# Attention on one core: score matmuls issued once, an order set by clocks kept for each engine, and a score tile read by two engines at once

## The chip, the cores and the metric

The kernel runs on one core of a Trainium2 chip. Its time is the device time of one execution in microseconds (us). Six runs of the kernel before gave a median of 2381.01 us, from 2344.32 to 2416.8. In what follows PE is the matrix engine, ACT is ScalarE, DVE is VectorE, POOL is GpSimd and SP the engine that issues most transfers.

## The reference

The input has 2048 rows of width 640. Two attention layers and two token-mixing layers alternate, each behind a layer norm and with a residual:

```python
def _A_ref(x, wqkv, wo):             # H = 32 heads, Dh = 20
    q, k, v = split_heads(x @ wqkv)
    scores = jnp.einsum("bhqd,bhkd->bhqk", q, k) * (Dh ** -0.5)
    p = softmax(scores, axis=-1)
    o = jnp.einsum("bhqk,bhkd->bhqd", p, v)
    return merge_heads(o) @ wo

def _B_ref(x, w1, b1, w2, b2):       # mixes along the 2048 rows, F = 1536
    u = gelu(jnp.einsum("bsd,sf->bdf", layernorm(x), w1) + b1)
    return (jnp.einsum("bdf,fs->bds", u, w2) + b2).transpose(0, 2, 1)

x = A_x
for _ in range(2):
    x = x + _A_ref(layernorm(x), A_wqkv, A_wo)
    x = x + _B_ref(layernorm(x), B_w1, B_b1, B_w2, B_b2)
```

The scores are the bulk of the work: 32 heads of 2048 by 2048 numbers in each layer, every one of which passes through an exponential.

## The kernel before

**Stages.** A prologue normalizes the input and projects V and the first keys and queries. Then come `attention` (line 247), the mixer's two halves `mixer_mm1` and `mixer_mm2` (lines 767 and 833), and the same three again for the second layer.

**A layer's attention.** Heads go in 8 groups of four (`g`), queries in 4 blocks of 512 (`qb`), keys in 16 blocks of 128 (`kt`). One *chunk* is the 128 x 512 scores of one head for one key block and one query block; it fills one PSUM bank. There are 2048 chunks, 64 for each of the 32 pairs of a query block and a head group; such a set of 64 is called a *group* below. Three chunks make a *score tile* `S` of three banks (683 tiles in a layer), and there are two such tiles (`sps`, line 251). The other two banks hold `acc`, which gathers probabilities times V for the running group (line 252), and `misc`, for all other matmuls (line 253).

For each tile the loop at lines 742 to 752 records, in this order: the score matmuls of the tile after it (`emit_S`, line 344), the exponential of this tile (`emit_exp`, line 415), some waiting work of DVE (`dve_run`, line 292), the matmuls with V that may go (`pv_ready`, line 675; called PV below), and some matmuls of the *fills* (`emit_fills`, line 714). Fills are all the other work that PE has to do under cover of the exponentials: projections of later keys and queries (line 230), the output projection (lines 553 and 587), and three quarters of the mixer's first product (line 525), whose partial sums are added up in DRAM by POOL's transfers (`uacc`, line 537). One fill group gathers in `misc` and is then copied out by DVE. The order in which the calls are made is the order of the instructions on PE (a chain, line 74) and on DVE (`manual_schedule`, line 740); ACT's exponentials follow it too.

**Two ways to take an exponential.** ACT takes whole tiles: one instruction at line 422 over two or three banks. For some tiles `want_dve` (line 360) leaves the third bank to DVE, which copies it scaled out of PSUM (`tp`, line 430) and, when two such chunks are there, runs five more instructions over both (lines 383 to 397) that build the exponential's bits in `PD`. Such a tile is called a *shared* tile here. A small model in the recording code, with clocks `act` and `dve` and costs in us written beside each operation, decides which tiles are shared and when DVE's waiting operations are recorded.

**What the score matmuls do.** A score matmul contracts over 20 of 32 rows, so heads sit in four strips of 32 rows of the array. Line 745 issues the three matmuls of each tile two or three times over, with the same operands and the same result:

```python
emit_S(t + 1, 2 if fill_queue or fill_state["cur"] else 3)
```

**At the end of a group** the finished `acc` is transposed by DVE out of PSUM (`T1`, line 445), which frees it for the next group, then divided by the row sums and transposed back (lines 452 to 459).

## Time and profile before

| what | value |
|---|---|
| median of 6 runs | 2381.01 us |
| the profiled execution | 2377.39 us, of which 2375.6 us lie between its first and last instruction |
| PE busy | 2095.8 us, 88% |
| ACT busy | 1827.6 us, 77% |
| DVE busy | 1590.7 us, 67% |
| mean granted PE clock | 0.925 of full speed |
| transfers | mean 41 GB/s |

In a profile a row names a line of the code, the engine, the operation, the tile written and the tile read, a count, the busy time and the mean of one, and then the time that the engine stood idle just before these instructions with what ended the wait. A busy PE is not PE at its best: matmuls overlap, and their ends are modelled, so the distance from one start to the next says what a matmul costs. The granted clock is the share of PE's full clock that its throttle let through.

### The profile page before, as it was taken

How to read it: one execution, taken by the hardware profiler on the slowest of the kernel's cores; microseconds unless marked ns; L12 is line 12 of the kernel's file. 1: busy time of each engine (PE TensorE's matmuls, PEld its weight loads, DVE VectorE, ACT ScalarE, POOL GpSimd, SP SyncE). 2: the span in 40 equal slices, each digit the busy share in tenths (PEclk: the TensorE clock that was granted, in tenths of full speed). 3: DMA queues.
4: the chain of work that ended last, by engine and by line, in shares of the span. 5: the costliest groups of instructions: out<-in, count | busy, mean ns of one | idle time of the engine just before them, and what ended most of it. 6: DMA issues, size and time to landing. Idle time of an engine off the chain costs nothing.

```text
span 2375.6 us, 41164 instructions
## 1 busy us (share of the span) xinstructions
PE 2095.8 (88%) x17114; PEld 644.7 (27%) x17284; DVE 1590.7 (67%) x2735; ACT 1827.6 (77%) x1504; POOL 157.0 (7%) x218
## 2 busy tenths in 40 slices
PE   7999999889888988888999899998998899888879
PEld 3222222222222222222542222222222222222235
DVE  6767777777656576656667677777566656766763
ACT  5888888888868787875358888888688677878862
POOL 2000001100120002000000000010001200021000
PEclk9999999999989799986999999999589867999989
DMA  4000002100240014103610000120002400132035
GB/s 115 1 1 1 1 16 73 47 1 21 55 73 1 1 40 70 16 1 99 211 54 1 1 1 1 41 80 27 1 17 65 78 1 1 45 64 33 1 111 174
DMA packets 90779, 97.47 MB, mean 41 GB/s; under 512 B 9696, under 2 KB 68192, under 8 KB 90592
## 3 DMA queue, kind: packets, MB, share of 16 engines
q1 hardware_dynamic: 70464, 71.22, 9.6%
q0 software_dynamic: 20128, 23.62, 6.3%
q8 instruction: 135, 2.21, 0.4%
q14 instruction: 52, 0.43, 0.1%
HBM read 55.48 MB, written 39.32 MB: 40 GB/s over the span
## 4 chain that ended last, share of the span: by engine, by line
PE 42%; ACT 19%; DVE 19%; issue 15%; POOL 4%; DMA 1%; ACTq 0%; POOLq 0%; SPq 0%; another core or an unknown queue 0%; DVEq 0%
PE S L340 20%; ACT P L422 19%; PE acc L654 9%; DVE tp L430 6%; PE y L879 4%; PE misc L230 3%; DVE PD L397 3%; PE misc L553 2%; PE pp L221 2%; POOL uacc_65 L537 1%; POOL uacc_66 L537 1%; PE big L808 1%; PE misc L525 1%; DVE KT L616 1%; DVE x1last L601 1%
## 5 line engine op out<-in xcount | busy, mean ns | idle before, releaser
L422 ACT ACTIVATE P<-S 128x1536 bf16<-128x1536 f32 (+1 forms) x1366 | 1735.6, 1313 | 384.9 <-PE S L340 372.9
L340 PE MATMUL S<-QTq,KT 32*128 32x512 bf16 x10020 | 1055.5, 409 | 138.2 <-DVE tp L430 93.1
L654 PE MATMUL acc<-P,Vaug 128*32 128x512 bf16 x3646 | 589.1, 413 | 35.7 <-DVE T_24414 L445 2.8
L340 PEld LDWEIGHTS <-KT 32*128 32x128 bf16 x10020 | 270.1, 95 | 654.0 <-issue 585.4
L430 DVE TENSOR_SCALAR tp<-S 128x512 f32<-128x512 f32 x450 | 307.0, 683 | 162.6 <-ACT P L422 160.9
L654 PEld LDWEIGHTS <-Vaug 128*32 128x32 bf16 x4096 | 146.4, 94 | 680.8 <-issue 679.8
L172 POOL TENSOR_TENSOR rstd<-veps,mhalf 128x1 f32<-128x1 f32 x64 | 41.7, 652 | 1807.4 <-DVE veps L167 1683.4
L532 DVE COPY ustg<-misc 128x512 f32<-128x512 f32 (+1 forms) x144 | 70.3, 488 | 130.0 <-PE misc L525 50.9
L525 PE MATMUL misc<-h2st,w1st 128*128 128x128 bf16 (+1 forms) x540 | 113.8, 310 | 35.9 <-DVE ustg L532 34.5
L654 PE MATMUL acc<-PD,Vaug 128*32 128x512 bf16 x450 | 116.6, 414 | 2.4 <-DVE PD L397 0.7
L879 PE MATMUL y<-uT,w2s 128*128 128x128 bf16 (+1 forms) x754 | 106.8, 297 | 3.1 <-ACT uT L822 2.4
L230 PE MATMUL misc<-hh,wq_pad 128*128 128x512 bf16 x278 | 90.3, 386 | 7.3 <-DVE QTq L616 4.5
L230 PE MATMUL misc<-hh,wk_pad 128*128 128x512 bf16 x240 | 79.2, 387 | 11.6 <-DVE KT L616 7.5
L553 PE MATMUL misc<-wo_pad,attnT 128*128 128x128 bf16 (+1 forms) x361 | 72.6, 299 | 2.5 <-issue 1.3
L879 PEld LDWEIGHTS <-w2s 128*128 128x128 bf16 x768 | 59.7, 98 | 48.9 <-issue 4.1
L525 PEld LDWEIGHTS <-w1st 128*128 128x128 bf16 x576 | 36.3, 98 | 101.9 <-issue 101.8
L616 DVE CAST QTq<-misc 128x512 bf16<-128x512 f32 x62 | 42.7, 688 | 18.7 <-PE misc L230 13.4
L84 ACT CAST Vaug<-pp 128x500 bf16<-128x500 f32 (+1 forms) x32 | 14.4, 454 | 53.0 <-PE pp L221 52.9
L221 PE MATMUL pp<-wv,hh 128*128 128x500 bf16 (+1 forms) x320 | 52.4, 315 | 1.7 <-DVE hh L86 1.7
L881 DVE SCALAR_TENSOR_TENSOR x2s<-y,b_t,x1in 128x512 f32<-128x512 f32 (+1 forms) x48 | 24.3, 548 | 42.0 <-PE y L879 24.6
L537 POOL DMA_DIRECT2D uacc_66<-ustg x48 | 42.9, 949 | 122.1 <-DVE ustg L532 121.9
L537 POOL DMA_DIRECT2D uacc_65<-ustg x48 | 42.5, 927 | 117.4 <-DVE ustg L532 117.2
(1518 smaller groups left out, 1582.8 us busy)
## 6 DMA issues: line engine op xcount, KB each, us to landing
w2s<-in_B_w_dram SPq DMA_DIRECT2D x16, 768.0 KB
w1st<-in_B_w_dram SPq DMA_DIRECT2D x36, 256.0 KB
uacc_65<-ustg POOLq DMA_DIRECT2D x36, 256.0 KB, 4.0
uacc_66<-ustg POOLq DMA_DIRECT2D x36, 256.0 KB, 4.1
xd_63<-x1s SPq DMA_DIRECT2D x24, 320.0 KB
x1in<-xd_63 SPq DMA_DIRECT2D x24, 320.0 KB
xd_64<-x2s SPq DMA_DIRECT2D x16, 320.0 KB
xin<-xd_64 SPq DMA_DIRECT2D x16, 320.0 KB
```

What stands on the lines that cost most here:

```text
L221: pe(nc.tensor.matmul(pp[:, 0:c1 - c0], lhsT=st.hT[:, dt_, tt * 128:(tt + 1) * 128], rhs=wv[:, dt_, c0:c1], start=(dt_ == 0), stop=(dt_ == ...
L230: pe(nc.tensor.matmul(t[:, :], lhsT=wpad[:, dt_, g, :], rhs=st.hT[:, dt_, tb * 512:(tb + 1) * 512], start=(dt_ == 0), stop=(dt_ == NDT - 1)))
L340: pe(nc.tensor.matmul(St[:, slot, :], lhsT=KT[32 * j:32 * j + 32, g, kt * 128:(kt + 1) * 128], rhs=get_QT(st, qb)[32 * j:32 * j + 32, g, : ...
L397: nc.vector.scalar_tensor_tensor(out=PD[:, 0:nb, :].rearrange("p a b -> p (a b)").bitcast(I16), in0=tp[:, 0:nb, :].rearrange("p a b -> p ( ...
L422: nc.scalar.activation(out=P[:, 0:na, :].rearrange("p a b -> p (a b)"), in_=St[:, 0:na, :].rearrange("p a b -> p (a b)"), func=ACT.Exp, sc ...
L430: nc.vector.tensor_scalar(out=batch["tp"][:, i, :], in0=St[:, 2, :], scalar1=SCALE * LOG2E * 128.0, scalar2=EXP_MAGIC, op0=ALU.mult, op1=A ...
L525: pe(nc.tensor.matmul(t[:, 0:w], lhsT=states[fp]["w"][:, sti, ftl * 128:(ftl + 1) * 128], rhs=tiles4[sti][:, c0:c1], start=(sti == 0), sto ...
L532: nc.vector.tensor_copy(out=stg[:, 0:w], in_=t[:, 0:w])
L537: nc.gpsimd.dma_start(out=dst, in_=stg[:, 0:w], accum_op=ALU.add)
L553: pe(nc.tensor.matmul(t[:, 0:w], lhsT=attnT[:, g, ttl * 128:(ttl + 1) * 128], rhs=wo_pad[:, g, c0:c1], start=(g == 0), stop=(g == NG - 1)))
L654: pe(nc.tensor.matmul(acc[32 * j:32 * j + 32, :], lhsT=Vaug[:, (kt * H + hh) * VW:(kt * H + hh) * VW + 32], rhs=rhs, start=(cnt[j] == 0), ...
L879: pe(nc.tensor.matmul(y[:, 0:w], lhsT=w2s[:, ft, sl * 128:(sl + 1) * 128], rhs=uT[:, ft, c0:c1], start=(ft == 0), stop=(ft == NF - 1)))
```

## The change

1. **Score matmuls once.** `emit_S(t + 1, 1)` for every tile. The program has 4096 score matmuls where it had 10020.
2. **Two readers at once.** The copy at line 430 is declared independent of the exponential at line 422. Both read the same score tile, but other banks of it.
3. **A clock for PE too.** The recording code now also follows PE (`clk["pe"]`, with a cost for every switch between the kinds of matmul), when each score tile is ready and when its slot is free. ACT's clock starts an exponential no earlier than its scores. Fills are recorded until PE's clock reaches the end of the running exponential (before: two matmuls' worth per tile), and no fill group starts whose `misc` bank the model has still in use.
4. **Smaller rules.** PV matmuls of ACT's chunks go once four are waiting. DVE's queued work is recorded until 0.4 us before the exponential's end. At most two pairs of DVE's chunks may be unfinished. `DVE_LAST` goes from 46 to 50. In the second layer `x1s` is written over `xin`, in three buffers.

The core of the diff:

```diff
-    FILL=2.0,
+    PV_BURST=4,
-    DVE_LAST=46,
+    DVE_LAST=50,
...
+            def pe_cost(mode, us):
+                if pe_mode[0] != mode:
+                    clk["pe"] += 0.1
+                    pe_mode[0] = mode
+                clk["pe"] += us
...
+                clk["pe"] = max(clk["pe"], slot_free.get(t - 2, 0.0) + 0.06)
+                pe_cost("S", 0.22 * passes)
+                s_done[t] = clk["pe"] + 0.16
...
+                if batch["tp"] is None and batch["unfinished"] >= 2:
+                    return False
...
+                clk["now"] = max(clk["act"], s_done.pop(t))
...
-                    dve_cost(0.66)
-                    nc.vector.tensor_scalar(out=batch["tp"][:, i, :], in0=St[:, 2, :], ...
+                    dve_cost(0.60)
+                    slot_free[t] = clk["dve"]
+                    cp = nc.vector.tensor_scalar(out=batch["tp"][:, i, :], in0=St[:, 2, :], ...
+                    tc.declare_no_dep(cp.ins, ex.ins, reason="disjoint PSUM banks of the score tile")
...
-                clk["act"] += 0.067 + 0.4267 * na
+                clk["act"] = clk["now"] + 0.067 + 0.4267 * na
+                slot_free[t] = max(clk["act"], slot_free.get(t, 0.0))
...
+                    burst = sum(len(x[2]) for x in pv_act if x[0] <= cur_t[0] - CFG["PV_LAGT"]) >= CFG["PV_BURST"]
...
-            def emit_fills(budget, pool_alloc):
+            def emit_fills(until, pool_alloc):
...
+                    nxt = (fs["cur"] or fill_queue[0])["cost"][fs["idx"] if fs["cur"] is not None else 0] * 0.22
+                    if until is not None and clk["pe"] + nxt + (0.1 if pe_mode[0] != "F" else 0.0) > until:
+                        break
...
+                        if until is not None and misc_free[0] > max(clk["pe"], clk["now"]) + 0.1:
                             break
...
-                        emit_S(t + 1, 2 if fill_queue or fill_state["cur"] else 3)
+                        emit_S(t + 1, 1)
...
-                    dve_run(clk["act"])
+                    dve_run(clk["act"] - 0.4)
                     pv_ready()
-                    emit_fills(CFG["FILL"], misc_alloc)
+                    emit_fills(clk["act"], misc_alloc)
```

**Where instructions move.** In the lists below a row is a line of the code, an operation, the tile it writes and the tiles it reads, and in brackets the engines whose signal it waits for. `s16`, `q16` and `PD` are the steps of DVE's exponential.

DVE inside a group of the first layer (second query block, no fills running), before:

```order
L394 TENSOR_TENSOR q16_6182<-q16_6182,s16_6181 128x1024 [waits DVE_49]
L430 TENSOR_SCALAR tp_6234<-S_6201 128x512 [waits Activation_49]
L430 TENSOR_SCALAR tp_6234<-S_6219 128x512 [waits Activation_49]
L397 SCALAR_TENSOR_TENSOR PD_6183<-tp_6163,q16_6182 128x1024 [waits DVE_49]
L383 TENSOR_SCALAR s16_6251<-tp_6234 128x1024 [waits DVE_49]
```

and after, in the same group, where fills (`ustg`) now run:

```order
L554 COPY ustg_4934<-misc_4929 128x128 [waits DMASW5_49,PE_49]
L450 TENSOR_SCALAR tp_4946<-S_4919 128x512
L450 TENSOR_SCALAR tp_4946<-S_4937 128x512 [waits PE_49]
L406 TENSOR_SCALAR s16_4886<-s16_4886 128x1024 [waits DVE_49]
L410 TENSOR_TENSOR q16_4887<-q16_4887,s16_4886 128x1024 [waits DVE_49]
L413 SCALAR_TENSOR_TENSOR PD_4888<-tp_4875,q16_4887 128x1024 [waits DVE_49]
```

The copy `tp` waited for ACT, that is for the exponential of the same tile; now it waits for PE, that is for the scores alone. It stays in DVE's one line of instructions, behind whatever stands there.

PE at a score tile whose slot a shared tile held, before. The last two rows are the first two of nine such pairs:

```order
L654 MATMUL acc_5720<-P_5847,Vaug_96 32x512
L340 LDWEIGHTS KT_100
L340 MATMUL S_5869<-QTq_3335,KT_100 128x512 [waits DVE_49]
L340 LDWEIGHTS KT_100
L340 MATMUL S_5869<-QTq_3335,KT_100 128x512
```

and after, with all of its score matmuls but one, left out at the dots:

```order
L351 LDWEIGHTS KT_100 [waits DVE_49]
L351 MATMUL S_6815<-QTq_3007,KT_100 128x512 [waits Activation_49]
L351 LDWEIGHTS KT_100
L351 MATMUL S_6815<-QTq_3007,KT_100 128x512
...
L677 LDWEIGHTS Vaug_96
L677 MATMUL acc_6819<-P_6800,Vaug_96 32x512 [waits PE_49]
```

A score tile is three matmuls where it was six or nine. Where DVE reads the slot too, PE now waits for both readers, DVE at the weights' load and ACT at the matmul; before, DVE's wait stood for both, since DVE came after ACT.

ACT where the group of the first fence ends, before:

```order
L422 ACTIVATE P_6437<-S_6409 128x1536 [waits PE_49,Activation_49]
L422 ACTIVATE P_6456<-S_6424 128x1024 [waits PE_49,Activation_49]
L422 ACTIVATE P_6475<-S_6439 128x1024 [waits PE_49,Activation_49]
L422 ACTIVATE P_6494<-S_6462 128x1536 [waits PE_49,Activation_49]
L422 ACTIVATE P_6511<-S_6482 128x1536 [waits PE_49,Activation_49]
```

and after:

```order
L440 ACTIVATE P_5057<-S_5041 128x1536 [waits PE_49,Activation_49]
L440 ACTIVATE P_5070<-S_5050 128x1536 [waits PE_49,Activation_49]
L440 ACTIVATE P_5076<-S_5059 128x1024 [waits PE_49,Activation_49]
L440 ACTIVATE P_5090<-S_5072 128x1024 [waits PE_49,Activation_49]
L440 ACTIVATE P_5102<-S_5080 128x1536 [waits PE_49,Activation_49]
```

`P_6437` and `P_5057` are the last tiles of the ending group, and in both programs DVE's list has that group's `T1` just ahead of the copies of the next shared tiles (`S_6424`, and `S_5059`). Before, the first shared tile stood right behind the group's last tile; after, there is one whole tile of ACT between them.

In the whole program ACT's exponentials are 914 over three banks and 452 over two before, 956 and 410 after; DVE copies 450 chunks before and 410 after. Of a layer's 683 tiles, 299 stood in runs of four or more without a fill, and now 124 do; the 48 wide matmuls of one quarter of the mixer's first product are spread over 36 to 46 tiles before and over 51 to 55 after.

More of the change, by code (lines that the diff above doesn't have):

```diff
@@ L273, in attention @@
             fill_state = dict(cur=None, idx=0, tile=None, unit=0)
-            clk = dict(now=0.0, act=0.0, dve=0.0)
+            clk = dict(now=0.0, act=0.0, dve=0.0, pe=0.0)
+            s_done = {0: 0.5}
+            slot_free = {}
+            misc_free = [0.0]
+            pe_mode = [None]
+            def pe_cost(mode, us):
[3 more added lines that the diff above has]
+                clk["pe"] += us
             dve_queue = deque()
@@ L720, in emit_fills @@
                             break
-                        if fill_queue[0].get("not_before", 0) > fs["unit"] and budget < 100:
+                        if until is not None and fill_queue[0].get("not_before", 0) > fs["unit"]:
+                            break
+                    nxt = (fs["cur"] or fill_queue[0])["cost"][fs["idx"] if fs["cur"] is not None else 0] * 0.22
+                    if until is not None and clk["pe"] + nxt + (0.1 if pe_mode[0] != "F" else 0.0) > until:
+                        break
+                    if fs["cur"] is None:
+                        if until is not None and misc_free[0] > max(clk["pe"], clk["now"]) + 0.1:
                             break
@@ L726, in emit_fills @@
                     grp = fs["cur"]
+                    pe_cost("F", nxt)
                     grp["mms"][fs["idx"]](fs["tile"])
-                    spent += grp["cost"][fs["idx"]]
                     fs["idx"] += 1
```

28 lines of the change are left out of this document (16 added, 12 removed).

## The prediction

> **What bounds the kernel now.** I read the page's head first, then the table of stages, the groups of instructions by shape, the waits, and last two stretches of the timeline.
>
> ```profile
> span 2375.6 us, 41164 instructions
> 50.00:1103.60 1053.60, 933.78 (x7804) 260.64 (x7871) 724.98 (x1183) 866.76 (x683) 65.56 (x84) 0.93 0.11 24
> 1223.00:2289.00 1066.00, 947.90 (x7805) 260.46 (x7872) 725.12 (x1183) 868.86 (x683) 65.36 (x84) 0.92 0.12 26
> ```
>
> The two rows are the attention stages: their length, then the busy time of PE, PE's weight loads, DVE, ACT and POOL, the granted clock, and the transfers' share and GB/s. They hold 1053.6 + 1066.0 = 2119.6 us. The other 256.0 us are not touched by the change. In attention ACT is busy 82% of the time and PE 89%, so neither is simply the limit.
>
> ```profile
> L422 ACT ACTIVATE P<-S 128x1536 bf16<-128x1536 f32 x914 | 1290.5, 1454 | 298.2 <-PE S L340 291.2 <-ACT P L422 0.3
> L422 ACT ACTIVATE P<-S 128x1024 bf16<-128x1024 f32 x452 | 463.5, 1028 | 86.7 <-PE S L340 81.6
> L340 PE MATMUL S<-QTq,KT 32*128 32x512 bf16 x10020 | 1055.5, 409 | 138.2 <-DVE tp L430 93.1 <-ACT P L422 30.0 <-issue 4.4
> ACT P L422 <- PE S L340: 372.9, 588, 4.2
> DVE tp L430 <- ACT P L422: 160.9, 194, 3.0
> DVE ustg L532 <- DMA uacc_66<-ustg: 44.3, 22, 4.9
> DVE ustg L532 <- DMA uacc_65<-ustg: 32.3, 14, 4.3
> PE misc L525 <- DVE ustg L532: 34.5, 38, 1.9
> ```
>
> ACT is idle for 384.9 us between its exponentials, and 372.9 of them are waits for score tiles. PE's waits for a slot say why: DVE's copies first, 93.1 us. Those copies wait 160.9 us for ACT. So a ring of three engines turns around two score tiles, and ACT, the engine with most necessary work, is its victim. A group without fills shows the ring:
>
> ```profile
> 501.67 0.69 DVE L430 TENSOR_SCALAR tp<-S 128x512 f32<-128x512 f32 x1 [0.74 <-ACT P L422]
> 502.42 0.83 PE L340 MATMUL S<-QTq,KT 32*128 32x512 bf16 x9 [0.49 <-DVE tp L430]
> 503.34 4.79 ACT L422 ACTIVATE P<-S 128x1536 bf16<-128x1536 f32 x4 [0.62 <-PE S L340]
> 508.76 11.51 ACT L422 ACTIVATE P<-S 128x1536 bf16<-128x1536 f32 x9 [0.62 <-PE S L340]
> 508.78 1.22 DVE L397 SCALAR_TENSOR_TENSOR PD<-tp,q_6252 128x1024 int16<-128x1024 f32 x1
> 519.51 0.72 DVE L445 STREAM_TRANSPOSE T_6452<-acc 128x512 f32<-128x512 f32 x1 [5.74 <-PE acc L654]
> 520.15 0.65 DVE L430 TENSOR_SCALAR tp<-S 128x512 f32<-128x512 f32 x1
> 520.86 0.82 PE L340 MATMUL S<-QTq,KT 32*128 32x512 bf16 x9 [1.39 <-DVE tp L430]
> 521.79 1.45 ACT L422 ACTIVATE P<-S 128x1536 bf16<-128x1536 f32 x1 [1.52 <-PE S L340]
> ```
>
> The copy starts when the exponential is over (501.67), the slot is free when the copy is over, PE writes nine matmuls (502.42), and only 0.92 us after their start does ACT go on. That is a stall of 0.62 us for a pair of shared tiles. At the group's end DVE stands 5.74 us before `T1`, the next copy queues behind it, and ACT loses 1.52 us (521.79). Where slots come in time ACT has no gap at all, in the nine tiles from 508.76.
>
> **The change, term by term.** All sums are in the profiled execution's span.
>
> *ACT's floor.* Two exponentials of two banks in a row show how far they overlap:
>
> ```profile
> 49.99 1.94 ACT L422 ACTIVATE P<-S 128x1024 bf16<-128x1024 f32 x2 [0.54 <-PE S L340]
> 1067.07 1.02 ACT L422 ACTIVATE P<-S 128x1024 bf16<-128x1024 f32 x1
> 1067.32 0.72 DVE L445 STREAM_TRANSPOSE T_12681<-acc 128x512 f32<-128x512 f32 x1 [5.75 <-PE acc L654]
> ```
>
> 1.94 - 1.02 = 0.92 us from start to start, an overlap of 0.11; so 1.454 - 0.11 = 1.345 us for three banks. After: 956 x 1.345 + 410 x 0.92 = 1663 us (before: 914 and 452 of them, 1645). DVE takes fewer chunks, which costs ACT 18 us. The nine tiles from 508.76, of which two are of two banks, should take 7 x 1.345 + 0.92 + 1.02 = 11.36 and took 11.51: 0.017 us a tile more, 23 us in all. That ACT and DVE read PSUM together is new only for one tile; the exponential at 1067.07 ran while DVE read `acc` and took its 1.02 us as ever. I put the price of two readers at 0.
>
> *The shared tiles.* With the copy beside the exponential a slot is free after 1.02 us instead of 1.02 + 0.69, and the third pass of score matmuls goes. The 0.62 us of a pair then vanish if DVE is free. It is in order, and its longest operation is 1.22 us (508.78). A copy stuck behind that is late by up to 1.22 us, on average 0.61, against some 0.5 us of slack in a two-bank tile. So a pair costs between 0 and 0.62 us; I take 0.25, nearer to the free end because the two copies of a pair now stand together in DVE's list with short operations around. 205 pairs: 51 us (0 to 125).
>
> *The group's end.* Before, 1.52 us. `T1` needs PE's last PV. After, one whole tile of ACT stands between the group's last tile and the first shared one, which is 1.345 us of room, and the restart needs one pass of score matmuls instead of three. I take 0.5 us, 64 times: 32 us (0.3 to 1.1, or 19 to 70).
>
> *Fewer matmuls, and PE's clock.* What they cost is read from starts, at full clock and at half:
>
> ```profile
> 163.75 0.40 PE L654 MATMUL acc<-P,Vaug 128*32 128x512 bf16 x3
> 164.07 0.39 PE L230 MATMUL misc<-hh,wq_pad 128*128 128x512 bf16 x1
> 164.40 0.82 PE L340 MATMUL S<-QTq,KT 32*128 32x512 bf16 x9
> 165.15 0.40 PE L654 MATMUL acc<-P,Vaug 128*32 128x512 bf16 x3
> 1072.09 1.46 PE L340 MATMUL S<-QTq,KT 32*128 32x512 bf16 x9
> 1073.48 0.61 PE L654 MATMUL acc<-P,Vaug 128*32 128x512 bf16 x3
> 1074.03 1.46 PE L340 MATMUL S<-QTq,KT 32*128 32x512 bf16 x9
> 786.80:790.20 3.40, 2.19 (x21) 0.72 (x21) 1.45 (x3) 2.62 (x3) 0.00 (x0) 1.00 0.00 0
> 790.20:824.30 34.10, 34.10 (x210) 6.85 (x207) 20.41 (x29) 21.96 (x17) 0.00 (x0) 0.50 0.00 1
> 834.60:838.00 3.40, 3.07 (x19) 0.50 (x17) 2.73 (x4) 1.95 (x2) 0.00 (x0) 0.50 0.02 5
> 836.79 0.63 PE L553 MATMUL misc<-wo_pad,attnT 128*128 128x512 bf16 x1 [0.33 <-issue]
> 838.00:845.00 7.00, 6.93 (x63) 2.02 (x60) 4.99 (x9) 5.71 (x5) 0.00 (x0) 1.00 0.00 1
> ```
>
> Full clock: PV of three 0.32 us, one fill 0.33, nine score matmuls 0.75. Half clock: 1.39 for nine and 0.55 for PV, 1.94 a tile. The three matmuls of a tile sit in different strips and run side by side, so nine are three passes, and a lone fill is one pass and a switch between kinds: (0.75 - 0.33) / 2 = 0.21 a pass, 0.12 a switch. One pass of scores is then 0.33, and at half clock 1.39 - 2 x 0.43 = 0.53. A tile after the change thus takes PE 0.65 us at full and 1.08 at half clock without fills, against ACT's 1663 / 1366 = 1.22. PE is not the limit there at either clock. And the clock will fall: it did so after the window at 786.8, in which PE was busy for 2.19 of 3.40 us, and stayed at 0.50 for 34 us while PE repeated its passes without a break. With a third of the score matmuls, stretches without fills will be at half clock. With fills it comes back: the first output projection at 836.79 stands in the window at 834.6, and from 838.0 the clock is full. So I charge 0.1 us for each of the 2 x 124 tiles in runs without fills, where 1.08 and bursts of five PV come close to 1.22: 25 us (0 to 60), and nothing where fills run.
>
> By the Trainium skill ("TensorE: Matmul & The Clock Gate", Part 1) the clock falls only after an idle window of about 3.4 us. The window at 786.8 was far from idle, so the trace disagrees and decides; by the page the 25 us would be 0.
>
> *Fills.* 36 tiles a quarter of the mixer's product become 51 to 55, so the transfers that add into DRAM come less often, and DVE's waits for them (44.3 + 32.3 = 76.6 us) should mostly go: I leave 15 (0 to 77). PE's waits for `misc` (34.5 us) stay in part: 25 (10 to 34). Start and drain of two layers: 6.
>
> *Sum.* 1663 + 23 + 51 + 32 + 25 + 15 + 25 + 6 = 1840 us of attention instead of 2119.6. With the 256.0 outside: 2096, and 2098 for the whole execution, whose time stands 1.8 above its span. The profiled execution lies 3.6 us below the runs' median, so a median of about **2100 us**, 12% less. All bounds at their low ends give 1722 + 256 = about 1980, all at their high ends 2058 + 256 = about 2315.
>
> **Rivals.**
>
> *A: ACT nearly without gaps.* Copies are never late and the transpose hides wholly: 0 for the shared tiles, 19 for group ends, 10 for fills. 1663 + 23 + 19 + 25 + 10 + 6 = 1746, or about 2005. For it speaks the gapless run of nine tiles; against it that DVE is busy 69% of attention in one line of instructions.
>
> *B: the copy's wait moves from ACT to DVE's own queue.* DVE's operations run later than the recording code thinks (it counts 1.17 for the one that took 1.22, and takes each of them to start on time), so slots stay held: 125 for the shared tiles, 70 for group ends, the rest as above: 1952, or about 2212. For it: copies stay in order. Against: DVE's list puts both copies of a pair together.
>
> *C: the stalls come back whole*, as waits of ACT for other reasons, such as PE held by a fill whose `misc` bank is late: about 2380, within 2%. Against it: so many necessary matmuls less.
>
> *D: slower, half clock under the fills.* The place is every tile with fills, 838 of 1366 by the order of the instructions. At half clock such a tile has 1.08 us of scores and PV; the 1118 wide and 528 narrow fills at 0.43 and 0.11 are 539 us, 0.64 a tile, and a switch 0.11: 1.83 us, more than ACT's 1.22. If all stayed cold: 838 x 1.83 + 528 x 1.22 + 32 = 2210, with 256 and the fills' 40 about 2506. It decides from about 280 us over my sum, at 0.61 a tile 460 tiles, 55% of those with fills. Against it: in the rows at 834.6 and 838.0 one window with fills brings the clock back.
>
> The Trainium skill speaks for D ("TensorE: Matmul & The Clock Gate", section "A second HAM failure mode: psum-queue depth-cycling"): short idle times of PE between groups of matmuls can make its clock swing and cost throughput. This trace shows the swing, and that tiles without fills bear it.
>
> **Chances.** Forecast 0.55 (its own range 2050 to 2160), A 0.12, B 0.21, C 0.06, D 0.06. The range leaves out C, D, the low part of A and the high part of B: 2015 to 2245. Faster by over 2% (about what a measurement of this kernel can tell from no change) are forecast, A and B: 0.88. Within 2% C: 0.06. Slower D: 0.06.
>
> **What would show it.** Right: copies wait for PE or nothing, and ACT's idle time for score tiles falls from 372.9 to about 150; PE's busy time falls far below 80% of attention; the clock is near 0.5 in runs without fills, near 1 with them; ACT's gap at a group's end is near 0.5. Wrong: PE slots still waiting on the copy (B), DVE still waiting for `uacc` transfers, or half clock in windows full of fills (D).

## The result, and the profile after

The changed kernel took 2007.07 us (median of 10 runs, 1999.72 to 2017.23); the kernel before took 2376.33 us (median of 20). The ratio, 0.850 with a 95% interval of 0.847 to 0.853, leaves out the runs of the kernel before that lie more than 1.5% above its fastest. That is 15% less, where 12% was forecast. Against the 2381 us of the prediction the ratio makes 2023 us, inside the range; the median itself lies 8 us under the low end. The profiled execution, which the rows and the account below show, took 1991.04 us, 16 us under the median.

The head of the page, and the table of the same three stages (first attention, between, second attention):

```profile
span 1989.3 us, 29161 instructions
49.03:917.30 868.27, 742.79 (x4843) 226.78 (x4912) 674.60 (x1103) 840.09 (x683) 62.29 (x84) 0.88 0.13 28
917.30:1035.60 118.30, 104.26 (x756) 60.55 (x768) 69.53 (x183) 40.70 (x59) 11.05 (x20) 0.94 0.58 185
1035.60:1901.60 866.00, 736.47 (x4842) 226.55 (x4912) 674.53 (x1103) 839.23 (x683) 62.30 (x84) 0.89 0.14 31
```

Attention takes 868.27 + 866.00 = 1734.3 us, 385 less than before; the rest of the span, 255.0, is what it was. ACT is now busy 97% of attention (82% before), PE 85% (89%). Three engines took turns; now one engine runs, and the others keep up with it. The groups of instructions by shape and the waits of the same kernel:

```profile
L440 ACT ACTIVATE P<-S 128x1536 bf16<-128x1536 f32 x954 | 1320.0, 1516 | 37.7 <-PE S L351 33.6
L440 ACT ACTIVATE P<-S 128x1024 bf16<-128x1024 f32 x412 | 421.9, 1103 | 18.3 <-PE S L351 17.0 <-ACT P L440 0.3
L351 PE MATMUL S<-QTq,KT 32*128 32x512 bf16 x4096 | 598.8, 425 | 229.7 <-ACT P L440 134.0 <-DVE tp L450 63.5 <-DVE QTq L638 3.0
ACT P L440 <- PE S L351: 50.5, 87, 2.6
DVE tp L450 <- PE S L351: 28.8, 46, 2.5
DVE ustg L554 <- DMA uacc_66<-ustg: 16.7, 9, 2.6
DVE ustg L554 <- DMA uacc_65<-ustg: 12.6, 7, 2.4
PE misc L547 <- DVE ustg L554: 4.5, 6, 1.1
```

Every wait that the prediction started from has shrunk, but for one. ACT's for scores went from 372.9 to 50.5 us. The copy's for ACT (160.9) is gone: it waits for PE, 28.8. PE's for the copy went from 93.1 to 63.5. PE now waits for ACT first, 134.0 (30.0 before), which is how it should be when ACT sets the pace. DVE's waits for the adding transfers went from 76.6 to 29.3, PE's for `misc` from 34.5 to 4.5.

**An account of ACT's time.** One number per kernel makes the experiments comparable. An exponential that follows another without a gap starts 1.331 us after it (three banks) or 0.904 (two banks): medians over the trace of the changed kernel. What a tile took beyond that, from its start to the next start, is its loss. The losses are summed over both layers and sorted by place: the first three tiles of a group (*turn*), other tiles at half clock while PE starts fills or not, and the rest at full clock. Shared tiles are counted as ACT's exponentials over two banks; one of them in each layer is its last tile, which has only two chunks. (By the trace the changed kernel has 954 exponentials over three banks and 412 over two, not 956 and 410.)

| kernel (span) | shared tiles a layer | turns | half clock, fills | half clock, none | rest | all |
|---|---|---|---|---|---|---|
| before (2375.6) | 226 | 159 | 18 | 98 | 220 | 494 |
| both parts, old order (2208.6) | 226 | 149 | 73 | 29 | 72 | 325 |
| + fill rule (2096.7) | 226 | 66 | 70 | 14 | 67 | 216 |
| + turn told (2036.4) | 204 | 31 | 52 | 12 | 42 | 137 |
| the changed kernel (1989.3) | 206 | 27 | 33 | 12 | 20 | 92 |

From row to row the losses fall by 169, 108, 79 and 46 us; a chunk given back to ACT costs it 0.427 us, so the third step pays 19 for 44 of them. The spans fall by 167, 112, 60 and 47. The account closes to within 4 us at each step. It is bookkeeping: it says where ACT's time went, not why.

### The profile page after: what moved, and what is told of

Read it like the earlier page. It is cut to its first block, busy times and chain, and to the rows that moved or that the text cites. A ratio compares the mean times of both kernels' runs of the same rounds, so it can differ in the third digit from the quotient of the medians.

```text
span 1989.3 us, 29161 instructions
## 1 busy us (share of the span) xinstructions
PE 1691.6 (85%) x11192; PEld 575.9 (29%) x11360; DVE 1489.5 (75%) x2575; ACT 1771.1 (89%) x1504; POOL 150.7 (8%) x218
## 4 chain that ended last, share of the span: by engine, by line
ACT 37%; PE 26%; issue 25%; DVE 8%; DMA 2%; POOL 2%; SPq 0%; another core or an unknown queue 0%; POOLq 0%; ACTq 0%; DVEq 0%
ACT P L440 36%; PE S L351 7%; PE acc L677 6%; PE y L911 5%; PE misc L230 3%; DVE tp L450 2%; PE pp L221 1%; PE big L840 1%; POOL uacc_65 L559 1%; DMA uacc_66<-ustg 1%; PE misc L547 1%; DVE QTq L638 1%; PE misc L609 0%; DVE bnst L161 0%; PE misc L575 0%
## 5 line engine op out<-in xcount | busy, mean ns | idle before, releaser
L440 ACT ACTIVATE P<-S 128x1536 bf16<-128x1536 f32 (+1 forms) x1366 | 1679.4, 1391 | 56.0 <-PE S L351 50.5
L351 PE MATMUL S<-QTq,KT 32*128 32x512 bf16 x4096 | 598.8, 425 | 229.7 <-ACT P L440 134.0
L677 PE MATMUL acc<-P,Vaug 128*32 128x512 bf16 x3686 | 602.4, 434 | 6.1 <-DVE T_17053 L467 1.6
L351 PEld LDWEIGHTS <-KT 32*128 32x128 bf16 x4096 | 195.4, 92 | 663.5 <-issue 462.6
L450 DVE TENSOR_SCALAR tp<-S 128x512 f32<-128x512 f32 x410 | 266.5, 679 | 29.3 <-PE S L351 28.8
L172 POOL TENSOR_TENSOR rstd<-veps,mhalf 128x1 f32<-128x1 f32 x64 | 36.9, 576 | 1332.4 <-DVE veps L167 917.9
L547 PE MATMUL misc<-h2st,w1st 128*128 128x128 bf16 (+1 forms) x538 | 119.6, 308 | 9.5 <-DVE ustg L554 4.5
L677 PE MATMUL acc<-PD,Vaug 128*32 128x512 bf16 x410 | 105.3, 433 | 1.7 <-DVE PD L413 1.4
L547 PEld LDWEIGHTS <-w1st 128*128 128x128 bf16 x576 | 38.2, 98 | 79.1 <-issue 76.6
L638 DVE CAST KT<-misc 128x512 bf16<-128x512 f32 x56 | 38.5, 688 | 17.4 <-PE misc L230 13.8
```

The costliest lines, as they stand in the source:

```text
L172: nc.gpsimd.tensor_tensor(out=rstd[:], in0=veps[:], in1=mhalf[:], op=ALU.pow)
L351: pe(nc.tensor.matmul(St[:, slot, :], lhsT=KT[32 * j:32 * j + 32, g, kt * 128:(kt + 1) * 128], rhs=get_QT(st, qb)[32 * j:32 * j + 32, g, : ...
L440: ex = nc.scalar.activation(out=P[:, 0:na, :].rearrange("p a b -> p (a b)"), in_=St[:, 0:na, :].rearrange("p a b -> p (a b)"), func=ACT.Ex ...
L450: cp = nc.vector.tensor_scalar(out=batch["tp"][:, i, :], in0=St[:, 2, :], scalar1=SCALE * LOG2E * 128.0, scalar2=EXP_MAGIC, op0=ALU.mult, ...
L547: pe(nc.tensor.matmul(t[:, 0:w], lhsT=states[fp]["w"][:, sti, ftl * 128:(ftl + 1) * 128], rhs=tiles4[sti][:, c0:c1], start=(sti == 0), sto ...
L638: nc.vector.tensor_copy(out=dst_ap, in_=t[:, :])
```

## The experiments

The prediction rests on a theory of the ring (R): the copy's wait and the second and third passes of score matmuls stand in ACT's way, and taking them out is the gain. Its rivals: the half clock that fewer matmuls bring eats the gain, the wait only moves into DVE's queue, or neither part matters much without the order (O). The letters stand for these in the expectations.

**The parts alone.** The kernel before with score matmuls once:

```diff
-                        emit_S(t + 1, 2 if fill_queue or fill_state["cur"] else 3)
+                        emit_S(t + 1, 1)
```

> The kernel before with each tile's score matmuls issued once and nothing else changed; the copy still waits for the exponential, and fills go two per tile. Theory R (a ring of two score tiles: the copy behind the exponential holds the slot, three passes of scores delay the refill): the stall of a pair of shared tiles falls from 0.62 to about 0.2 us, a group's end from 1.52 to about 1.1, and the half-clock stretches of 1.94 us a tile fall to ACT's pace. 225 x 0.43 + 64 x 0.42 + about 100 = 225 us less: a time near 2150. Rival K (the repeated passes held PE's clock up, and fills at half clock make PE the limit): no gain or a loss, 2370 or more, with a granted clock near 0.5 in windows with fills.

The kernel before with two readers at once:

```diff
+                    tc.declare_no_dep(cp.ins, ex.ins, reason="disjoint PSUM banks of the score tile")
```

> The kernel before with the copy declared independent of the exponential and nothing else changed; score matmuls still go two or three times. Theory R: warm pairs lose most of their 0.62 us (225 x 0.5 = 110 us less), group ends keep 1.52, half-clock stretches keep PE's 1.94 us a tile: near 2265. Rival W (the second reader is the whole of the gain): near 2020. Rival Q (the copy's wait only moves into DVE's own line of instructions): near 2376, with PE still waiting for the copy about as long as before.

Both, in the old order:

> The kernel before with both: scores once and the copy beside the exponential; the old order rules. Theory R: the two parts add, and the new order is worth the rest: 2376 - 225 - 60 = about 2090, so that the order's share of the 357 us is about 70. Rival O (the order by clocks carries the gain): 2200 or more. Rival N (the order gives nothing): 2020.

Measured: 2269.97 us for the first (ratio 0.964, 0.961 to 0.968), 2315.07 for the second (0.984, 0.980 to 0.989), 2212.65 for both (0.940, 0.936 to 0.944). The groups of ACT and of the copy, of the first and then of the second:

```profile
L422 ACT ACTIVATE P<-S 128x1536 bf16<-128x1536 f32 (+1 forms) x1366 | 1707.0, 1316 | 310.2 <-PE S L340 303.4 <-ACT P L422 0.7
L430 DVE TENSOR_SCALAR tp<-S 128x512 f32<-128x512 f32 x450 | 306.4, 682 | 80.8 <-ACT P L422 78.4
```

```profile
L422 ACT ACTIVATE P<-S 128x1536 bf16<-128x1536 f32 (+1 forms) x1366 | 1728.7, 1314 | 329.7 <-PE S L340 317.5 <-ACT P L422 0.2
L430 DVE TENSOR_SCALAR tp<-S 128x512 f32<-128x512 f32 x450 | 303.2, 679 | 47.5 <-PE S L340 43.8
```

In the second kernel the copy no longer waits for ACT at all, and ACT still waits 317.5 us for scores, against 372.9. Taking a wait away is not the same as taking the loss away: DVE comes to the copy when its list lets it, not when the data is there. Both parts together are worth 6% of the 15%. R's numbers fell (near 2150, near 2265 and about 2090), O stands: the order by clocks brings 2213 to 2007, 206 us. Half clock does not eat the gain either: the mean granted clock of the first kernel is 0.772, against 0.925 before, and it is 3.6% faster.

**The changed kernel without two readers.** All of the change, but the copy waits for the exponential:

```diff
-                    tc.declare_no_dep(cp.ins, ex.ins, reason="disjoint PSUM banks of the score tile")
```

> The changed kernel without the declaration: the copy waits for the exponential again, all else as after, with a model that does not know of the wait. Theory R: a pair of shared tiles stalls ACT by 0.2 to 0.4 us again, 206 x 0.3 = 60 us, and the copies behind it run late: 2070 to 2110. Rival (with one pass of scores there is slack enough for a copy behind the exponential): 2010 to 2030.

Measured: 2097.73 us, 0.891 (0.886 to 0.895).

```profile
L440 ACT ACTIVATE P<-S 128x1536 bf16<-128x1536 f32 (+1 forms) x1366 | 1700.5, 1336 | 142.5 <-PE S L351 138.6 <-ACT P L440 1.3
L450 DVE TENSOR_SCALAR tp<-S 128x512 f32<-128x512 f32 x410 | 281.6, 689 | 148.1 <-ACT P L440 146.3
```

That is in the range that R gave. The same line was worth 1.6%, some 37 us, in the kernel before, and 2.4%, 57 us, in the old order with scores once (2269.97 to 2212.65); in the new order it is worth 4.1%, 91 us. The 91 us are what it costs to break an order that was made for the early copy, since the model does not know of the wait; what an order made for the waiting copy would lose was not tried. The parts are not additive: the early copy is worth most where the order counts on it.

**The changed kernel with the passes back**, two where fills are pending and three elsewhere, the model not told of them:

```diff
-                        emit_S(t + 1, 1)
+                        emit_S(t + 1, 2 if fill_queue or fill_state["cur"] else 3)
```

> The kernel after with the second and third pass of the score matmuls put back (two where fills are pending, else three), the clock model not told of them, so that the order of the instructions is that of the kernel after. PE is 85% busy in its attention stages at a mean granted clock of 0.89; the 4866 added matmuls are about 1620 passes, at 0.21 us a pass 340 us of PE. Theory P (a pass stands between a free slot and ACT's next tile, as in the old order, where taking them out was worth 0.964 of the time): 2070 to 2140 us, ACT's idle time for scores over 100 us instead of 50.5. Theory N (the order hides them, and they keep the clock up): 2000 to 2030 us, ACT's idle time for scores below 70 us. If PE has become the bound outright (1470 + 340 us in 1734 us, less what a full clock gives back): 2100 to 2200 us and PE above 95% in attention.

Measured: 2058.54 us, 0.872 (0.865 to 0.880), between the theories. The score group of PE and the first attention stage:

```profile
L351 PE MATMUL S<-QTq,KT 32*128 32x512 bf16 x8964 | 891.2, 379 | 111.7 <-DVE tp L450 51.2 <-ACT P L440 48.9 <-DVE QTq L638 4.6
48.60:948.80 900.20, 841.73 (x7347) 225.80 (x7343) 675.58 (x1103) 852.30 (x683) 62.38 (x84) 1.00 0.13 28
```

The clock is full in both attention stages, 1.00, and the kernel is 51 us slower than at 0.88. PE is not saturated either, 842 of 900 us. The passes still stand between a free slot and ACT's next tile: ACT's idle time for scores is 87.8 us instead of 50.5. They cost 51 us; in the old order they cost 102 with two readers (2315.07 to 2212.65) and 85 (3.6%) with one. The new order hides a part of them, no more.

**The half clock.** The changed kernel has stretches without fills at half clock. One second pass there, 778 matmuls more, warms them (the model again not told):

```diff
-                        emit_S(t + 1, 1)
+                        emit_S(t + 1, 1 if fill_queue or fill_state["cur"] else 2)
```

> The kernel after with one second pass of score matmuls, only where no fills are pending (776 matmuls), the clock model not told of it. There the kernel after runs at a granted clock of 0.5 and ACT loses 46 us in two layers against its pitch. Theory C (the half clock costs this): if the passes keep the clock up, 1965 to 1990 us. Theory H (half clock does no harm where PE is not the limit, the loss has another cause): 1995 to 2020 us, not to be told from the kernel after; if the clock stays at 0.5 nevertheless, two passes at half clock take PE about 1.5 us a tile against ACT's 1.22 and it gets slower, 2020 to 2060 us.

Measured: 1987.04 us (1968.12 to 1992.99), 0.840 (0.835 to 0.846). That is 1% under the changed kernel, and the fastest one of this study; the two intervals lie close, and the two were not timed side by side. By the number theory C is right; the trace says something narrower. The same stretch of the first layer in the windows, of the changed kernel and then of this one:

```profile
442.90:475.00 32.10, 29.83 (x151) 6.41 (x150) 22.59 (x34) 31.60 (x27) 0.00 (x0) 0.50 0.00 1
```

```profile
440.00:480.00 40.00, 31.59 (x287) 9.45 (x284) 31.07 (x48) 39.87 (x34) 0.38 (x1) 1.00 0.05 15
```

The clock went from 0.50 to 1.00, and ACT was busy 31.60 of 32.10 us there before, so little was to be won in the stretch itself. What half clock costs shows where fills start again. ACT and then PE of the changed kernel around such a place:

```profile
693.27 7.89 ACT L440 ACTIVATE P<-S 128x1536 bf16<-128x1536 f32 x6 [0.21 <-PE S L351]
701.76 1.45 ACT L440 ACTIVATE P<-S 128x1536 bf16<-128x1536 f32 x1 [0.60 <-PE S L351]
703.82 1.02 ACT L440 ACTIVATE P<-S 128x1024 bf16<-128x1024 f32 x1 [0.60 <-PE S L351]
706.15 9.08 ACT L440 ACTIVATE P<-S 128x1024 bf16<-128x1024 f32 x7 [1.30 <-PE S L351]
```

```profile
695.15 0.61 PE L351 MATMUL S<-QTq,KT 32*128 32x512 bf16 x3
695.69 0.61 PE L677 MATMUL acc<-P,Vaug 128*32 128x512 bf16 x3
696.28 0.61 PE L351 MATMUL S<-QTq,KT 32*128 32x512 bf16 x3
...
701.05 0.61 PE L351 MATMUL S<-QTq,KT 32*128 32x512 bf16 x3
701.59 0.61 PE L677 MATMUL acc<-P,Vaug 128*32 128x512 bf16 x3
702.13 1.03 PE L575 MATMUL misc<-wo_pad,attnT 128*128 128x512 bf16 x2
703.10 0.61 PE L351 MATMUL S<-QTq,KT 32*128 32x512 bf16 x3
```

Without fills a tile is 0.54 us of scores and 0.54 to 0.59 of PV, ready before ACT's 1.331 is over, and six exponentials follow without a gap. From 701.05 to 703.10 the tile holds two fills too, 2.05 us. ACT stands 0.60 us before each of two exponentials and 1.30 before the third; the clock comes back at 705.8, and the third and six more run without a gap. The model in the recording code counts a fill at full clock, 0.22 us; here the two took 0.97. Over both layers 66 such tiles lose 33 us, 0.50 each, while 183 tiles at half clock without fills lose 12 us, 0.07 each. In the profiled execution of the kernel with the second pass the half-clock tiles outside the turns are 108 instead of 249, but those with fills still 55 and 27 us; all losses together are 95 us. Its 1% is therefore measured and not explained: that execution, of 1992.95 us at clock 0.945, is among its slowest runs and no shorter than the profiled one of the changed kernel (1991.04), so that no trace here shows the gain. The fastest run, 1968.12, had clock 0.969.

**The fill rule.** The changed kernel with the old budget of two matmuls after each tile, whatever PE's clock and `misc` say:

```diff
-                    emit_fills(clk["act"], misc_alloc)
+                    emit_fills_old(2.0)
```

> The kernel after, but fills are given out by the old rule: two matmuls after each tile, whether PE's clock in the model has room and whether the buffer misc is free or not. Theory F (the spreading of fills carries a good part of the 205 us between the old order and the new one): 2050 to 2090 us, DVE's waits for the transfers that add the mixer's pieces back from 29 towards 80 us and PE's waits for DVE's evacuation of misc back over 30 us. Theory T (the group's turn carries it, fills do not matter): 2000 to 2025 us, these waits may be back but ACT's idle time for scores stays below 70 us.

And the reverse, the old order with only the new fill rule (the rules for shared tiles, DVE's list and PV as before):

> The kernel with both parts of the change, the old rules for DVE's list, the shared tiles and the PVs, and of the new order only the rule for the fills: PE's clock in the model and the buffer misc decide when a fill is given out. Its first tile is shared in 24 of 32 groups, 226 shared tiles a layer as in the old order. The old order took 2213 us; with the new order but the old fill rule it was 2077, with both new 2007, so that the fill rule was worth 70 us there. If the two add up: 2125 to 2160 us, ACT's idle time for scores 150 to 200 us. Theory F (the fill rule carries most by itself): 2030 to 2090 us. Theory T (without the new rules for the turn it is worth little): 2185 to 2215 us.

Measured: 2076.6 us (0.879, 0.873 to 0.885) without the rule, so it is worth 70 us there; 2105.63 us (0.895, 0.889 to 0.901) with the rule alone, so it is worth 107 us in the old order. The first is what theory F gave; the second lies between F and the two rules adding up, so that each half of the order does a part of the other's work. The waits of the old order with both parts, then of the old order with the rule:

```profile
ACT P L422 <- PE S L340: 249.5, 340, 4.1
DVE ustg L533 <- DMA uacc<-ustg: 85.9, 42, 6.0
PE misc L526 <- DVE ustg L533: 51.2, 40, 4.0
```

```profile
ACT P L438 <- PE S L351: 160.5, 227, 3.7
DVE ustg L551 <- DMA uacc<-ustg: 29.2, 10, 5.4
PE misc L544 <- DVE ustg L551: 12.0, 12, 3.2
```

PE stands 12.0 us before a `misc` bank that DVE has not emptied, instead of 51.2, and DVE 29.2 us before a transfer, instead of 85.9. Most of the gain is not there but in the turns, 149 to 66 us, which is 83 of the 108 us by which the losses fall. `T1` starts a median 0.81 us after the end of the group's last exponential instead of 1.25, and the traces show three things that go together there. They are counted over the 62 turns between two groups of a layer.

- *Fewer fills in the way.* In the old order 29 turns have a fill on PE between the group's last exponential and `T1`. They lose 3.0 us each, the others 1.9. With the rule 28 turns have one, and lose 0.8 each.
- *The clock.* In the old order 32 turns begin at half clock, with the rule 5; the mean clock of the profiled executions goes from 0.782 to 0.896. In turns without such a fill `T1` starts a median 1.25 us after the exponential's end at half clock and 0.81 at full clock, in both kernels.
- *The place.* A finished fill now moves DVE's clock in the model, and by that the first tile is no longer shared in 16 turns. 14 of these lose 0.1 us each.

What each of the three is worth was not separated. The kernel with the rule also has `x1s` over `xin` in the second layer, as the changed kernel has. The losses fall by 44 us in the first layer, which has no such edit, and by 64 in the second, so that at most some 20 of the 107 us can belong to it.

**The turn of a group.** Two edits that move the place of the first shared tile and little else (6 and 12 shared tiles a layer fewer). In the changed kernel every group's first tile is shared, as before:

```diff
+                if pos < 5:
+                    return True
```

> The kernel after with one rule added: the first score tile of every group of 64 chunks is shared with DVE, as in the kernel before (32 of 32 groups a layer, instead of 3 of 32); the second shared tile is then the third one as a rule, the others stand as they are, 200 instead of 206 a layer. The six chunks fewer a layer cost ACT 12 x 0.43 = 5 us. Theory T (the turn of a group carries most of the 205 us: the copy of a tile stands in DVE's list behind T1, which waits for PE's last PV, and ACT waits for the slot): 58 of 64 turns get 1 to 2 us longer, 2070 to 2130 us, ACT's idle time for scores 110 to 170 us instead of 50.5. Theory F (the fills carry it): 2005 to 2030 us.

In the old order with both parts, no group's first tile is shared:

```diff
-                if pos > CFG["DVE_LAST"] or pos < 2:
+                if pos < 5 or pos > CFG["DVE_LAST"] or pos < 2:
```

> The kernel with both parts of the change and the old order (2213 us), with one rule added: the first score tile of a group is not shared with DVE, so that the first shared tile is the second one in all groups (214 shared tiles a layer instead of 226, which costs ACT 24 x 0.43 = 10 us). There ACT lost 72 and 75 us a layer on the first three tiles of its groups. Theory T (the place of the first shared tile decides that loss): it falls to 25 to 45 us a layer, 2130 to 2170 us. Theory I (the turn is late because PE is late with the group's last PV, behind fills that the old rule gives out without regard to PE, so that the place alone helps little; the reverse edit in the new order was worth 36 us): 2175 to 2215 us.

Measured: 2042.89 us (0.865, 0.859 to 0.871) for the first, 36 us slower than the changed kernel and short of what theory T gave; 2223.68 us (0.945, 0.938 to 0.951) for the second, no gain, as theory I had it (24 chunks given back to ACT are 10 of the 11 us more). By tile of the group the old order loses 9, 49 and 14 us on the first three in the first layer; with the first not shared 3, 31 and 42. The loss moved with the shared tile. So the place matters once the rest is in step, and by itself it is worth nothing: the theory that the place decides fell.

Then the old order with the fill rule, and one line more, by which the model knows that `T1` waits for PE:

```diff
-                dve_cost(0.75)
+                clk["dve"] = max(clk["dve"], clk["pe"] + 0.16)
+                dve_cost(0.60)
                 nc.vector.transpose(out=T1[:], in_=acc[:])
```

> The kernel with only the fill rule of the new order (2106 us) and one rule of the new order more: DVE's clock in the model waits for PE's last PV before the group's T1. By that the first tile of a group is shared in 1 of 32 groups instead of 24, and 204 tiles a layer are shared instead of 226 (19 us more for ACT: 44 x 0.43). What is then left between this kernel and the new one are the 0.4 us that DVE's list stays behind ACT's clock, the bursts of four PVs, ACT's clock waiting for the scores and three small numbers. Theory T (that the model knows when T1 can start carries most of the 98 us still open): 2005 to 2045 us, ACT's idle time for scores 50 to 90 us instead of 160. Theory S (the shorter list of DVE carries it): 2075 to 2115 us, idle time for scores above 110 us. Half and half lies between.

Measured: 2041.4 us (0.867, 0.862 to 0.871), 64 us for one rule, at the upper end of theory T's range. It moves the first shared tile from the first to the second or third place (first place in 1 of 32 groups instead of 24) and, since the model now knows that DVE loses time there, it shares 204 tiles instead of 226. What the turn looks like, first in the old order with both parts, then in the changed kernel, both without a fill at the turn (ACT's rows, then DVE's, and in the second PE's):

```profile
483.79 3.34 ACT L422 ACTIVATE P<-S 128x1536 bf16<-128x1536 f32 x3
488.62 2.93 ACT L422 ACTIVATE P<-S 128x1536 bf16<-128x1536 f32 x2 [1.49 <-PE S L340]
486.55 0.72 DVE L446 STREAM_TRANSPOSE T<-acc 128x512 f32<-128x512 f32 x1 [6.03 <-PE acc L655]
487.19 0.65 DVE L430 TENSOR_SCALAR tp<-S 128x512 f32<-128x512 f32 x1
```

```profile
473.03 1.99 ACT L440 ACTIVATE P<-S 128x1024 bf16<-128x1024 f32 x2
475.46 2.91 ACT L440 ACTIVATE P<-S 128x1536 bf16<-128x1536 f32 x2 [0.44 <-PE S L351]
474.86 0.72 DVE L467 STREAM_TRANSPOSE T_5318<-acc 128x512 f32<-128x512 f32 x1 [1.62 <-PE acc L677]
475.50 0.65 DVE L450 TENSOR_SCALAR tp<-S 128x512 f32<-128x512 f32 x1
473.78 1.03 PE L677 MATMUL acc<-PD,Vaug 128*32 128x512 bf16 x2
474.74 0.61 PE L351 MATMUL S<-QTq,KT 32*128 32x512 bf16 x3
```

In the old order DVE has stood 6.03 us before `T1`, the copy behind it starts at 487.19, and ACT waits 1.49 us for the slot that this copy frees. In the changed kernel DVE stood 1.62 us, ACT had a tile of its own to go on with, and waited 0.44. That wait is not for the copy behind `T1`, which starts at 475.50, when ACT has gone on; it is for scores that stood on PE behind the ending group's last PVs (473.78, then 474.74). Over all turns of the changed kernel 24 of the 27 us are lost at the third tile, 18 of them where PE waited for a copy before it wrote the next scores.

**More sharing.** ACT is the limit, DVE has a fifth of its time free. Does it pay to give DVE more? DVE's list is recorded up to ACT's clock instead of 0.4 us before it, and no tile is shared before the ninth chunk:

```diff
-                    dve_run(clk["act"] - 0.4)
+                    dve_run(clk["act"])
...
-                if pos > CFG["DVE_LAST"] or pos < 2:
+                if pos > CFG["DVE_LAST"] or pos < 8:
```

> The kernel after with two numbers changed: DVE's list is filled up to ACT's clock instead of 0.4 us before it, and no tile is shared before the ninth chunk of a group. 242 shared tiles a layer instead of 206, the first of them the third tile of its group. ACT's floor falls by 72 x 0.43 = 31 us, DVE gets 72 x 2.3 = 166 us more (now 1350 of 1734 us in attention). Theory A (ACT is the bound now, DVE and PE have room): 1960 to 1985 us. Theory D (at 87% DVE's list is so full that copies come late): 2005 to 2050 us, ACT's idle time for scores over 90 us instead of 50.5.

Measured: 2038.7 us (0.867, 0.863 to 0.871), 32 us slower, with 242 shared tiles: theory D.

```profile
L440 ACT ACTIVATE P<-S 128x1536 bf16<-128x1536 f32 (+1 forms) x1366 | 1659.6, 1336 | 129.7 <-PE S L351 124.4 <-ACT P L440 0.5
PE acc L677 <- DVE PD L413: 18.8, 49, 0.9
```

ACT is busy 20 us less and idle 74 us more. PE waits 18.8 us for `PD`, which it waited for 1.4 us in the changed kernel: DVE's results come late, and the shared tiles' slots too. The edit changes two numbers, and 72 shared chunks follow from them; what each does was not separated. The later place is not the harm: the turns lose 7.5 us instead of 27. The tiles at full clock outside the turns lose 93 instead of 20.

## Why the prediction was right, and where its sum was off

**Direction and end state: right. Source of the gain: in part.** The bound was the ring of three engines, the copy's wait went, and ACT became the engine that sets the pace. But scores once and two readers alone bring 6 of the 15%, and the order, which the forecast gave small parts of its terms, brings the rest. The sum was 107 us too long, 2096 against a span of 1989.3. Rival A, ACT nearly without gaps, at 2005, describes the outcome better than the forecast did. Its 1746 us of attention against 1734 measured came with other parts, though. The 2023 us lie below the forecast's own range, 2050 to 2160, in the part of the stated range that was left to A. All errors of the sum but one point the same way, so they hardly cancelled. Term by term:

| term | forecast | measured |
|---|---|---|
| ACT's floor and residual | 1663 + 23 | 1642 (954 x 1.331 + 412 x 0.904) |
| shared tiles | 51 | 18 |
| group ends | 32 | 27 |
| half clock without fills | 25 | 12 |
| half clock with fills | 0 | 33 |
| `uacc`, other waits, start and drain | 15 + 25 + 6 | 2 |

*The floor, 44 us off.* The counts were 954 and 412 instead of 956 and 410, which is 1 us; the rest is the pitch. In the kernel before three banks took 1.347 us from start to start (median), and the 1.345 of the forecast was a good reading of it. In the changed kernel they take 1.331, and the residual per tile is gone. In both kernels the tile right after a gap takes a median 1.348 us to the next start and, from the third tile of a run on, 1.331; but 760 exponentials began after a gap before, and 175 after. The exponentials also overlap more: over three banks one lasts a mean 1.516 us instead of 1.454. A pitch read where an engine often starts from a stop is not the pitch of the same engine when it never stops.

*Shared tiles, 33 us off.* The step that failed says that a copy stuck behind DVE's 1.22 us operation is late by up to that. In the changed kernel copies are seldom late enough to matter: PE waits 63.5 us for them in all, and ACT loses 18 us at shared tiles. The new order keeps the list shorter, at most two unfinished pairs and 0.4 us behind ACT, which would explain it and was not tested by itself. With more chunks on DVE the forecast's loss does appear: 63 us in the kernel with 242 shared tiles, at full clock, on the tiles with two banks and the next ones.

*Group ends.* 0.5 us each were forecast, 0.42 measured (27 us in 64). The reason was incomplete: the forecast gave it to the tile that ACT has in between. The place alone, tried in the old order, brought nothing. Under the fill rule it pays: the turns lose 66 us, and 31 once the model knows of `T1`.

*Fills, 44 us off.* The forecast saw fewer waits for `uacc` (76.6 to 29.3) but charged ACT for what was left. DVE and PE still have them, and ACT does not feel them. That the fill rule is a main part of the change, 70 to 107 us, the prediction did not see: it gave fills a side term, and counted all its gain on the ring.

*Half clock, in the wrong place.* The charge of 25 us was put on tiles without fills; they lost 12. "Nothing where fills run" was wrong by 33 us. Rival D's mechanism, fills at half clock, does occur, for some tiles each time that fills start again, then the clock returns; its 1.83 us for a mean tile stands beside 2.05 for the tile with two fills above. For the kernel as a whole D did not occur. By the Trainium skill ("TensorE: Matmul & The Clock Gate", section "A second HAM failure mode: psum-queue depth-cycling") throughput suffers when the clock swings between bursts. The 33 us agree with that, in a kernel that got 15% faster at a lower clock.

*Signs that were misjudged.* "PE's busy time falls far below 80% of attention": it fell by 402 us, from 1881.7 to 1479.3, and is 85%, since attention shrank as well and matmuls at half clock are longer. The sign should have been given in us. Two more signs came out between right and wrong. ACT's idle time for scores was to fall to about 150 us and is 50.5. PE still waits 63.5 us for the copy, as rival B has it, but 93.1 before.

**How the gain divides.** Scores once alone 3.6%, two readers alone 1.6% (2.4% on top of scores once), both 6.0%. Fill rule on top of these 4.5% of the time before, the turn told to the model 2.8%, all other rules together 1.7%. The order of the steps matters: the two halves of the order overlap (70 to 107 us for the fill rule), and two readers are worth more at the end than at the start.

**What stays open.** The last 40 us belong to several small rules (the 0.4 us, bursts of PV, ACT's clock waiting for scores, the limit of two pairs, later last shared tiles) that were not separated; only for the 0.4 us is there a run, and it moves the first shared tile and shares more. How much of the fill rule's worth is the clock, which it raises in both orders (0.782 to 0.896, and 0.809 to 0.894), is open. The new order without the line on `T1` was not tried. What the second pass gains its 1% by is open.

## What to carry to other kernels

When in-order engines pass tiles around, removing a dependency frees time only if the instruction behind it comes up at that moment; here, with scores once in both, the freed copy was worth 2.4% in an order that did not know the engines' clocks and 4.1% in one that did. Build such an order on a model of every engine in the ring, above all of waits that one engine's list has for another, and hold optional work to what the engine has room for until the next necessary piece. Do not fill the helper engine's list for its own sake: here a list without 0.4 us of slack and 72 chunks more for DVE cost 32 us, though they took work off the engine that is the limit.

## What the runs showed of the hardware

- PE fell to half clock without a long idle time: in the changed kernel it was busy 2.13 us of the 3.40 before the fall (439.50 to 442.90, clock 1.00), with no idle time over 0.62 us. In the stretch from 442.90 the busy time is 29.83 of 32.10 us at a granted clock of 0.50, with matmuls that use 32 rows or 32 columns of the array. A second pass of the same 32-row matmuls kept it at 1.00. By the Trainium skill ("TensorE: Matmul & The Clock Gate", section "HAM oscillation — how this bites in real kernels") it is idle gaps of over about 3.4 us that bring the clock down; this trace disagrees.
- Half clock cost ACT little where PE had room: 183 tiles at half clock without fills lost 0.07 us each, 66 with fills 0.50.
- ACT and DVE read two banks of one tile at the same time at no price. In the kernel before with two readers, 221 two-bank exponentials that began after a gap with a copy beside them took a median 1.024 us, 32 such without one 1.024 us.
